# Two row blocks of the last batch moved into the second group of rows, and row scales per two blocks

## The chip, the cores and the metric

The kernel runs on one core of one Trainium2 chip. The metric is the device time of one execution in microseconds, from the runs of the kernel; the profile is one further execution with the hardware profiler on. PE is the matrix engine (PEld its weight loads), DVE the vector engine, ACT the scalar engine, POOL GpSimd, SP the engine that issues the DMAs.

## The reference, cut to what matters

Two stages, for 4 batches, 8 heads of 64 columns and 768 positions. The first is a decayed linear attention; its output, all heads side by side, is `x` of 4 x 768 x 512. The second mixes `x` by a Fourier transform and sends it through a small network:

```python
# first stage, per batch and head, over t:
state = gamma * state + outer(k[t], v[t]);  y[t] = scale * q[t] @ state
# second stage:
X = np.fft.fft(x, axis=1); X = np.fft.fft(X, axis=2)
u  = x + np.real(X)
un = (u - mean(u)) / np.sqrt(var(u) + 1e-06)      # over the 512 columns
out = u + np.maximum(un @ w_ch1, 0.0) @ w_ch2     # 512 -> 2048 -> 512
```

## The kernel before

The 768 rows of a batch are six blocks of 128 rows (`kb` 0 to 5). The program is one core's, and for the last batch the order of the work is set in three steps: lists of units ("streams") are given a start and an end in units of one batch; `emit` sorts all units by their times, which fixes the order in which they are written down; a scheduler under it then sets each engine's instruction order, near to the written one. Each engine then works strictly in its order, and an instruction waits by semaphores for what it reads and for the buffers that it overwrites.

The units that the change and the prediction speak of, with the lines of the kernel before:

- `s2_unit(b, kb)` makes `u` of one block: four matmuls `pq` (L1010), two ACT copies `qn` of the sine parts (L1012, L1013), two DVE instructions that put the parts together (L1017, L1020), and two POOL additions of `x` (L1038, L1040). It is the last step of the Fourier transform. Blocks 3 to 5 are the mirror images of the first three in the sequence's frequencies.
- `norm_unit(b, kb)`: statistics of `u` on DVE (L1050, L1051), then `un = mean - u` on ACT in 16 bits (L1052). It is not divided by the deviation here.
- `unT_unit(b, kb)`: a transposing DMA of `un` into `unT`, issued by SP (L1071).
- `rstd_unit(b, rt)`: the row scales, 1/sqrt(var + eps), by a Sqrt on ACT (L1062) and a reciprocal on DVE (L1064), of three blocks at a time. The scale is applied where the network's output is added to `u`.
- `ch_unit`: the second matrix product of the batches before the last, with L1131 on DVE as its end.

The last batch has no attention work of a next batch beside it. Its network runs over three groups `g` of two blocks each (256 rows), and the second matrix product is done by seven products of half size instead of eight:

- `hp_unit(b, g, n)`, n = 0 to 7: eight matmuls (L1175) into one of three PSUM buffers (`psh`, pool `ps_pm`), then a Relu on ACT (L1180); for n = 7 the second half of the Relu is on DVE (L1183). After n = 2, 5 and 7 DVE makes four sums and differences of the results (L1193).
- `p_unit(b, g, k)`, in the order k = 1, 4, 5, 6, 2, 7, 3: eight matmuls (L1217) and the additions into `u` or into the output buffer on DVE (L1222). Products 1 and 2 share a PSUM bank, so do 6 and 7, and 5 and 3; the second of a pair is accumulated on the first's result after DVE has read that. Stores to `out` go through SP.

```python
# the last batch, before:
for g in range(3):
    majors += [hp_unit(b, g, n) for n in range(8)]
    if g < 2:
        majors.append(rstd_unit(b, g))
    majors += [p_unit(b, g, k) for k in (1, 4, 5, 6, 2, 7, 3)]
```

In the kernel before, blocks 3, 4 and 5 of every batch are put down by `mix_units` with the times `DM1`: for the last batch their three `s2_unit` fall between the hp units of group 0, each norm follows the next block's `s2_unit`, and all is done within group 0. Blocks 0 to 2 are made during the batch before. Group 0 reads blocks 0 and 1, group 1 blocks 2 and 3, group 2 blocks 4 and 5.

Of the kernel before, what the change touches and what calls it, by code (L numbers as in the profile page):

```python
# [20 lines left out]
B, H, S, D = 4, 8, 768, 64  # L21
# [28 lines left out]
DM0, DM1 = (0.183, 0.205, 0.286, 0.408), (0.004, 0.137, 0.232, 0.341)  # L50
# [4 lines left out]
HT0 = (0.666, 0.693, 0.632, 0.590)  # L55
NPE = 2
WS = (-0.12, -0.02)
KD = (2, 3)
NT = 0.6
ACT_ROWS = ((2, 5, 6, 7, 8, 9, 10, 14), (0, 3, 6, 7, 9, 10, 11, 12, 14, 15))  # L60
# [3 lines left out]
def kernel(  # L64
# [330 lines left out]
    for j in range(2):  # L395
# [6 lines left out]
        t = const.tile([P, 257], f32, tag=f"qn_{j}", name=f"qn_{j}", padded_shape=[P, 260])  # L402
# [201 lines left out]
    def t_unit(b, i):  # L604
        def run():
# [9 lines left out]
            for dst, src in ((qT, q16_of[b, i]), (kT, kd_of[b, i])):  # L615
                if dst is kT and i in KD:
                    nc.sync.dma_start_transpose(kT, src.rearrange("p c h d -> p (c h d)"))
# [248 lines left out]
    def g0_unit(b, parts=(0, 1, 2)):  # L866
        def run():
            for part in parts:
                (g0_a, g0_b, g0_c)[part](b)
        return run  # L870
# [79 lines left out]
    def bn_unit(kb):  # L950
        def run():
            stats = lb[0]["st"]
            bst = stt.tile([P, 6], f32, tag=f"bst{kb % 3}", name="bst")
            nc.vector.bn_stats(bst, lb[0]["u"][:, kb, :])
            nc.vector.bn_aggr(stats[:, kb, 0:2], bst)
        return run
# [87 lines left out]
    def norm_unit(b, kb):  # L1044
        def run():
            u, stats = lb[b]["u"], lb[b]["st"]
            bst = stt.tile([P, 6], f32, tag=f"bst{kb % 3}", name="bst")
            un = unp.tile([P, 2, 257], f16, tag="un16", name="un16").rearrange(
                "p a b -> p (a b)")[:, 0:DM]
            nc.vector.bn_stats(bst, u[:, kb, :])  # L1050
            nc.vector.bn_aggr(stats[:, kb, 0:2], bst)  # L1051
            nc.scalar.activation(un, u[:, kb, :], AF.Identity, bias=stats[:, kb, 0:1], scale=-1.0)  # L1052
            lb[b]["un", kb] = un
        return run

    def rstd_unit(b, rt):
        def run():
            stats = lb[b]["st"]
            if b == 0 and rt == 0:
                bn_unit(0)()  # L1060
            sl = slice(3 * rt, 3 * rt + 3)
            nc.scalar.activation(stats[:, sl, 2:3], stats[:, sl, 1:2], AF.Sqrt, bias=epsT,  # L1062
                                 scale=1.0)
            nc.vector.reciprocal(out=stats[:, sl, 3:4], in_=stats[:, sl, 2:3])  # L1064
        return run

    def unT_unit(b, kb):
        def run():
            un, unT = lb[b].pop(("un", kb)), lb[b]["unT"]
            if b > 1 or b and kb >= 3:  # L1070
                nc.sync.dma_start_transpose(unT[:, :, kb * P:(kb + 1) * P], un)  # L1071
                return
            pst = ps_g.tile([P, 4, P], f16, tag="g", name="pst", padded_shape=[P, 8, P])
            for cb in range(4):
                nc.tensor.transpose(pst[:, cb, :], un[:, cb * P:(cb + 1) * P], ident16)
            if (kb % 2 == 0) != (b == 0 and kb < 3):
                nc.vector.tensor_copy(unT[:, :, kb * P:(kb + 1) * P], pst)
            else:
                nc.scalar.copy(unT[:, :, kb * P:(kb + 1) * P], pst)
        return run  # L1080
# [84 lines left out]
    def hp_unit(b, g, n):  # L1165

        def run():
            unT = lb[b]["unT"]
            if (g, n) == (0, 0):
                seven["s4"] = spare(8 * P, "s4").rearrange("p (n k) -> p n k", n=8)  # L1170
            psh = ps_pm.tile([P, 2, 256], f32, tag="pm", name="psh")
            for t in range(2):
                fb = n + 8 * t
                for cb in range(4):
                    nc.tensor.matmul(psh[:, t], w116[:, cb, fb * P:(fb + 1) * P],  # L1175
                                     unT[:, cb, g * 256:(g + 1) * 256],
                                     start=(cb == 0), stop=(cb == 3))
            for t0, t1, eng in (((0, 1, "a"), (1, 2, "v")) if n == 7 else ((0, 2, "a"),)):
                if eng == "a":
                    nc.scalar.activation(hg[:, n, t0:t1], psh[:, t0:t1], AF.Relu, bias=0.0,  # L1180
                                         scale=-1.0)
                else:
                    nc.vector.tensor_scalar(out=hg[:, n, t0:t1], in0=psh[:, t0:t1], scalar1=-1.0,  # L1183
                                            scalar2=0.0, op0=ALU.mult, op1=ALU.max)
            if n in (2, 5, 7):
                sl = slice({2: 0, 5: 3, 7: 6}[n], n + 1)
                a11, a12 = hg[:, sl, 0, 0:P], hg[:, sl, 1, 0:P]
                a21, a22 = hg[:, sl, 0, P:256], hg[:, sl, 1, P:256]
                s1, s2, s4 = sg[:, 0, sl], sg[:, 1, sl], seven["s4"][:, sl]
                for out_, x, y, op in ((s1, a21, a22, ALU.add), (s2, s1, a11, ALU.subtract),  # L1190
                                       (s4, a12, s2, ALU.subtract),
                                       (a21, a11, a21, ALU.subtract)):
                    nc.vector.tensor_tensor(out=out_, in0=x, in1=y, op=op)  # L1193
        return run
# [167 lines left out]
    def mix_units(b, kbs, s0, s1, u0, u1):  # L1362
        def turn(j):
            def run():
                s2_unit(b, kbs[j])()
                if j:
                    norm_unit(b, kbs[j - 1])()
            return run
        t = s1 + NT * min((s1 - s0) / 3, u1 - s1)
        return [([turn(j) for j in range(3)], s0, s1), ([norm_unit(b, kbs[2])], t, t),  # L1370
                ([unT_unit(b, kb) for kb in kbs], u0, u1)]
# [21 lines left out]
    streams = []  # L1393
    for b in range(B):
        majors = []
        if b == B - 1:
            for g in range(3):
                majors += [hp_unit(b, g, n) for n in range(8)]
                if g < 2:
                    majors.append(rstd_unit(b, g))  # L1400
                majors += [p_unit(b, g, k) for k in (1, 4, 5, 6, 2, 7, 3)]
            streams.append(([held(wsum_unit(k, part)) for part in range(2) for k in (1, 2, 3, 4)],
                            b + WS[0], b + WS[1]))
        elif b == 0:
            for kb in range(3):
                if kb:
                    majors.append(unT_unit(0, kb))
                majors += [h0_unit(kb, g) for g in range(4)]
        else:
            majors += [h_unit(b, 0, fb) for fb in range(NFB)]  # L1410
        if b < B - 1:
            majors.append(rstd_unit(b, 0))
            majors += [ch_unit(b, 0, rb3, part) for rb3 in range(3) for part in range(4)]
            majors += [h_unit(b, 1, fb) for fb in range(NFB)]
            majors.append(rstd_unit(b, 1))
            majors += [ch_unit(b, 1, rb3, part) for rb3 in range(3) for part in range(4)]
        streams.append((majors, b, b + 1.0))
        streams += mix_units(b, [3, 4, 5], *(b + t for t in (DM0 if b == 0 else DM1)))
        if b + 1 < B:
            steps = attn_steps(b + 1)  # L1420
            if b == 0:
                streams.append(([load_unit(1, i, 6) for i in range(4)], LD0[0], LD0[1]))
                streams.append(([qt_zeros], 0.1, 0.15))
                streams.append(([half_tables], HT0[0], HT0[1]))
                streams.append(([pad_unit], HT0[2], HT0[3]))
                ts = TS0
            else:
                streams.append(([load_unit(b + 1, i) for i in range(4)], b + LD1[0], b + LD1[1]))
                n = [len(u) for u in steps[1:]]
                ts = list(TS1[:2]) + [TS1[2] + TS1[3] * sum(n[:j]) / sum(n) for j in range(6)]  # L1430
            streams.append((steps[0], b + ts[0], b + ts[1]))
            streams += [(u, b + ts[j + 2], b + ts[j + 3]) for j, u in enumerate(steps[1:])]
            end = b + ts[-1]
            da = DA0 if b == 0 else DA1
            sums = [s1_unit(b + 1, e, cb) for cb in range(2) for e in range(2)]
            sums.insert(1, g0_unit(b + 1, (1, 2)))
            streams.append((sums, end + da[0], end + da[1]))
            streams += mix_units(b + 1, [0, 1, 2], *(end + t for t in da[2:]))
# [31 lines left out]
```

## Time and profile before

| what | value |
|---|---|
| median of 3 runs | 241.73 us (241.58 to 241.75) |
| the profiled execution | 241.30 us |
| its span, first to last instruction | 239.4 us |
| PE busy | 226.8 us, 95% |
| DVE busy | 189.6 us, 79% |
| ACT busy | 125.2 us, 52% |
| POOL busy | 81.6 us, 34% |
| granted TensorE clock | 0.998 |

The span is counted from the first instruction; all times in the views are us from there. A line of a timeline gives start, length, engine, source line, operation, output and inputs, form, count, and in brackets the idle time of the engine before it with what ended that. An instruction's length is from its start to its last write; the next on the same engine starts a little before that end.

### The profile page before, as it was taken

What the parts mean: (1) busy time and instruction counts of PE and PEld (TensorE: products, weight loads), DVE (VectorE), ACT (ScalarE), POOL (GpSimd) and SP (SyncE); (2) the same over time, 40 slices, a digit from 0 to 9 for tenths busy, and PEclk for the clock granted to TensorE, in tenths of its full rate; (3) what the DMA queues carried; (4) which work ended last, traced back from release to release, by engine and by line L of the source; (5) the groups of instructions that cost most, each with busy time, mean ns of one, the idle gap of its engine ahead of it and who ended that gap; (6) DMA issues with size and microseconds to landing.
All of it is one profiled execution on the core that took longest, in us unless ns stands there. A gap on an engine that the chain in (4) does not pass through costs nothing.

```text
span 239.4 us, 5574 instructions
## 1 busy us (share of the span) xinstructions
PE 226.8 (95%) x2127; PEld 155.5 (65%) x2127; DVE 189.6 (79%) x472; ACT 125.2 (52%) x272; POOL 81.6 (34%) x148
## 2 busy tenths in 40 slices
PE   0899999999999999999999999999999998999994
PEld 0376779756775646765567446655675476788883
DVE  8789987968898889986995739977886888848473
ACT  5989758675865544841248406822356337152430
POOL 8378802575300097850001817930003203200000
PEclk9999999999999999999999999999999999999999
DMA  7999999999999289979999487675100240220202
GB/s 181 231 271 238 231 206 208 220 250 248 251 222 227 49 196 213 198 144 136 258 279 216 96 184 204 130 121 153 44 3 0 71 131 22 47 88 1 90 0 88
DMA packets 101242, 36.78 MB, mean 154 GB/s; under 512 B 91489, under 2 KB 98529, under 8 KB 101217
## 3 DMA queue, kind: packets, MB, share of 16 engines
q1 hardware_dynamic: 96992, 32.25, 63.4%
q0 software_dynamic: 4224, 4.19, 10.6%
q8 instruction: 16, 0.26, 0.5%
q14 instruction: 10, 0.07, 0.1%
HBM read 27.26 MB, written 6.29 MB: 140 GB/s over the span
## 4 chain that ended last, share of the span: by engine, by line
PE 85%; DVE 7%; ACT 2%; DMA 2%; issue 1%; POOL 1%; SPq 0%; DVEq 0%; ACTq 0%
PE psc L1127 25%; PE psh L1088 21%; PE psh L1175 7%; PE ps L1217 7%; PE psh L1105 3%; PE wkA L665 3%; PE ps L848 3%; PE ps L828 2%; PE wkY L719 2%; DMA k<-in_k_dram 2%; PE pq L1010 1%; PE wkY L715 1%; PE wkK L684 1%; PE wps L172 1%; PE pq L922 1%
## 5 line engine op out<-in xcount | busy, mean ns | idle before, releaser
L1127 PE MATMUL psc<-w,ht 128*128 128x512 f16 x288 | 67.7, 379 | 0.0
L1088 PE MATMUL psh<-unT,w 128*128 128x384 f16 x320 | 59.5, 326 | 0.0
L1038 POOL TENSOR_TENSOR u<-u,x 128x256 f32<-128x256 f32 x21 | 13.3, 635 | 109.9 <-DVE u L1017 97.5
L1127 PEld LDWEIGHTS <-ht 128*128 128x128 f16 x288 | 27.3, 98 | 26.5
L1088 PEld LDWEIGHTS <-w 128*128 128x128 f16 x320 | 29.9, 98 | 15.9 <-DMA unT<-un 0.4
L1092 ACT ACTIVATE ht<-psh 128x384 f16<-128x384 f32 x46 | 22.3, 489 | 23.4 <-PE psh L1088 22.7
L668 DVE TENSOR_TENSOR atm<-wkA,maskp 128x512 f16<-128x512 f32 x36 | 23.6, 683 | 1.5 <-PE wkA L665 1.5
L1180 ACT ACTIVATE ht<-psh 128x512 f16<-128x512 f32 (+1 forms) x24 | 13.7, 570 | 20.2 <-PE psh L1175 20.2
L1052 ACT ACTIVATE un<-u,stats 128x512 f16<-128x512 f32 x21 | 14.8, 719 | 14.2 <-DVE stats L1051 8.3
L1175 PE MATMUL psh<-unT,w 128*128 128x256 f16 x192 | 22.3, 273 | 0.0
L1094 DVE TENSOR_SCALAR ht<-psh 128x384 f16<-128x384 f32 x34 | 18.7, 551 | 2.7 <-PE psh L1088 2.5
L1175 PEld LDWEIGHTS <-w 128*128 128x128 f16 x192 | 18.7, 98 | 2.3
L1131 DVE SCALAR_TENSOR_TENSOR ob<-psc,stats,u 128x512 f32<-128x512 f32 x18 | 13.4, 744 | 8.2 <-PE psc L1127 7.9
L694 DVE SCALAR_TENSOR_TENSOR s<-s,gk,wkK 128x128 f16<-128x128 f16 x48 | 16.2, 338 | 2.4 <-ACT s L690 1.6
L727 ACT ACTIVATE x<-wkY,gexp 128x384 f16<-128x384 f32 x24 | 12.9, 580 | 9.0 <-PE wkY L719 8.9
L1050 DVE BATCH_NORM_STATS2 bst<-u 128x6 f32<-128x512 f32 x21 | 14.4, 688 | 3.9 <-POOL u L1040 3.7
L1217 PEld LDWEIGHTS <-ht 128*128 128x128 f16 x144 | 13.7, 98 | 4.0 <-ACT ht L1180 1.8
L1193 DVE TENSOR_TENSOR ht<-ht 128x384 f16<-128x384 f16 (+1 forms) x27 | 8.8, 353 | 8.3 <-ACT ht L1180 8.0
L439 POOL TENSOR_SCALAR kd<-k,gexp 128x384 f16<-128x384 f32 x24 | 13.8, 585 | 3.7 <-DMA k<-in_k_dram 3.5
L1040 POOL TENSOR_TENSOR u<-u,x 128x256 f32<-128x256 f32 x21 | 13.4, 640 | 0.0
L665 PE MATMUL wkA<-qTz,kT 128*128 128x256 f16 x72 | 13.2, 272 | 0.0
L1217 PE MATMUL ps<-wsum,ht 128*128 128x256 f16 x96 | 11.8, 273 | 0.1
(190 smaller groups left out, 398.7 us busy)
## 6 DMA issues: line engine op xcount, KB each, us to landing
q<-in_q_dram SPq DMA_DIRECT2D x16, 384.0 KB, 6.0
k<-in_k_dram SPq DMA_DIRECT2D x16, 384.0 KB, 5.7
v<-in_v_dram SPq DMA_DIRECT2D x16, 384.0 KB, 5.9
out_dram<-ob SPq DMA_DIRECT2D x21, 256.0 KB, 2.7
w<-in_moe_w_ch_dram POOLq DMA_DIRECT2D x8, 512.0 KB, 10.8
out_dram<-ob SPq DMA_DIRECT2D x5, 128.0 KB, 2.0
unT<-un SPq DMA_TRANSPOSE x15, 2.5
kT<-kd SPq DMA_TRANSPOSE x10, 2.9
```

The lines of the kernel that those rows point to most:

```text
L439: kc = nc.gpsimd.tensor_scalar(out=kd[:, :, h2, :], in0=k32[:, h2], scalar1=gkd[:, h0 + h2:h0 + h2 + 1], scalar2=1.0, op0=ALU.mult, op1=AL ...
L665: mm = nc.tensor.matmul(wk[:, c2], st["kT"][:, c, :], st["qT"][:, :, c, :], start=True, stop=True)
L668: nc.vector.tensor_tensor(out=st["atm"][:, 2 * part:2 * part + 2], in0=wk, in1=maskp[:, PAIR_ORDER[i]].unsqueeze(1).to_broadcast([P, 2, 2, ...
L694: nc.vector.scalar_tensor_tensor(out=s16[:, c], in0=s16[:, c - 1], scalar=gk2[:, hp:hp + 1], in1=wk[:, c - c0], op0=ALU.mult, op1=ALU.add)
L1050: nc.vector.bn_stats(bst, u[:, kb, :])
L1052: nc.scalar.activation(un, u[:, kb, :], AF.Identity, bias=stats[:, kb, 0:1], scale=-1.0)
L1088: nc.tensor.matmul(psh, w116[:, cb, fb * P:(fb + 1) * P], unT[:, cb, rt * 384:(rt + 1) * 384], start=(cb == 0), stop=(cb == 3))
L1092: nc.scalar.activation(ht16[:, fb, :], psh, AF.Relu, bias=0.0, scale=-1.0)
L1094: nc.vector.tensor_scalar(out=ht16[:, fb, :], in0=psh, scalar1=-1.0, scalar2=0.0, op0=ALU.mult, op1=ALU.max)
L1127: nc.tensor.matmul(psc, ht16[:, fb, rb3 * P:(rb3 + 1) * P], w216[:, fb, :], start=(fb == 0), stop=(fb == NFB - 1))
L1175: nc.tensor.matmul(psh[:, t], w116[:, cb, fb * P:(fb + 1) * P], unT[:, cb, g * 256:(g + 1) * 256], start=(cb == 0), stop=(cb == 3))
L1217: nc.tensor.matmul(ps[:, c0:c1], lhsT, rhs[:, c0:c1], start=bool(new and n == 0), stop=(n == 7), skip_group_check=True)
```

## The change

In the last batch blocks 3, 4 and 5 no longer come from `mix_units`: each unit gets a time of its own. One batch is 48 units long there (three times 8 hp, one scale unit, 7 products), so block 3's `s2_unit` at 0.02 stands ahead of the first hp unit, its norm at 0.06 after the second, its transpose at 0.15; block 4's `s2_unit` at 0.36 stands after the first hp unit of group 1, its norm at 0.41 and transpose at 0.50; block 5's at 0.42, 0.47 and 0.56. The row scales of the last batch are made for two blocks at a time, three times, after the hp units of each group; before, they were made for three blocks, twice.

```diff
+LAST_MIX = {3: (0.02, 0.06, 0.15), 4: (0.36, 0.41, 0.50), 5: (0.42, 0.47, 0.56)}
...
-    def rstd_unit(b, rt):
+    def rstd_unit(b, rt, n=3):
...
-            sl = slice(3 * rt, 3 * rt + 3)
+            sl = slice(n * rt, n * rt + n)
...
                 majors += [hp_unit(b, g, n) for n in range(8)]
-                if g < 2:
-                    majors.append(rstd_unit(b, g))
+                majors.append(rstd_unit(b, g, 2))
                 majors += [p_unit(b, g, k) for k in (1, 4, 5, 6, 2, 7, 3)]
...
-        streams += mix_units(b, [3, 4, 5], *(b + t for t in (DM0 if b == 0 else DM1)))
+        if b < B - 1:
+            streams += mix_units(b, [3, 4, 5], *(b + t for t in (DM0 if b == 0 else DM1)))
+        else:
+            streams += [([unit(b, kb)], b + t, b + t) for kb, ts in LAST_MIX.items()
+                        for unit, t in zip((s2_unit, norm_unit, unT_unit), ts)]
```

## The prediction

> **What bounds the kernel now.** I read the page, then the stages of the last batch by window, then the timelines of PE, ACT, DVE and POOL there. The page's first lines and its row of transposes:
>
> ```profile
> span 239.4 us, 5574 instructions
> PE 226.8 (95%) x2127; PEld 155.5 (65%) x2127; DVE 189.6 (79%) x472; ACT 125.2 (52%) x272; POOL 81.6 (34%) x148
> ...
> unT<-un SPq DMA_TRANSPOSE x15, 2.5
> ```
>
> PE is the bound, so only PE's gaps and PE's instruction count can move the time. The count stays (the same matmuls in another order). The windows, cut at the three groups of rows (stage, length, then busy PE, PEld, DVE, ACT, POOL):
>
> ```profile
> 193.68:209.44 15.76, 14.33 (x133) 12.11 (x132) 13.09 (x35) 7.70 (x18) 3.80 (x6) 1.00 0.18 47
> 209.44:222.54 13.10, 13.10 (x122) 11.71 (x120) 8.33 (x22) 4.55 (x8) 0.00 (x0) 1.00 0.13 46
> ```
>
> PE's timeline (start, length, count, idle before):
>
> ```profile
> 193.68 1.91 PE L1175 MATMUL psh<-unT,w 128*128 128x256 f16 x16
> 195.43 0.40 PE L1010 MATMUL pq<-gk,g16r 128*128 128x129 f16 x4
> 195.66 1.91 PE L1175 MATMUL psh<-unT,w 128*128 128x256 f16 x16
> ...
> 202.49 0.28 PE L1217 MATMUL ps<-w,ht 128*128 128x256 f16 x1 [0.31 <-ACT ht L1180]
> 203.76 0.28 PE L1217 MATMUL ps<-w,ht 128*128 128x256 f16 x1 [0.99 <-ACT ht L1180]
> ...
> 209.77 6.82 PE L1175 MATMUL psh<-unT,w 128*128 128x256 f16 x61
> 216.43 1.04 PE L1217 MATMUL ps<-w,ht 128*128 128x256 f16 x8
> ...
> 222.54 7.15 PE L1175 MATMUL psh<-unT,w 128*128 128x256 f16 x64
> ```
>
> Group 1 is gapless: 64 matmuls of hp and 56 of p in 13.10 us, 0.109 each. (Three of its 64 run inside group 0, hence 209.77 - 3 x 0.109 = 209.44.) A block's four pq matmuls take 195.66 - 195.43 = 0.23. So group 0's 15.76 us is 13.10 + 3 x 0.23 + **1.96 us of waiting**, and the change can win no more. Who is waited for:
>
> ```profile
> 194.76 0.60 ACT L1180 ACTIVATE ht<-psh 128x512 f16<-128x512 f32 x1 [5.20 <-PE psh L1175]
> 195.63 0.60 ACT L1180 ACTIVATE ht<-psh 128x512 f16<-128x512 f32 x1 [0.28 <-PE psh L1175]
> 196.12 0.27 ACT L1012 COPY qn<-pq 128x128 f32<-128x128 f32 x1
> 196.27 0.29 ACT L1013 COPY qn<-pq 128x127 f32<-128x127 f32 x1
> ...
> 200.90 0.72 ACT L1052 ACTIVATE un<-u,stats 128x512 f16<-128x512 f32 x1 [0.71 <-DVE stats L1051]
> ...
> 202.72 0.72 ACT L1052 ACTIVATE un<-u,stats 128x512 f16<-128x512 f32 x1 [0.28 <-issue]
> 203.35 0.36 ACT L1180 ACTIVATE ht<-psh 128x256 f16<-128x256 f32 x1
> ```
>
> ACT works in order. A block's `un` waits there for its DVE and POOL chain, and the Relus of hp stand behind it: the Relu of n=7 ends at 203.71 and PE goes on at 203.76.
>
> **The change part by part.** Read from the changed program's instruction order. PE: block 3's pq, 64 hp, 56 p; then 8 hp, pq 4, 24 hp, pq 5, 32 hp, 56 p; group 2 as before. ACT from group 0 on (Relus by n):
>
> ```
> g0: qn3 | R0 R1 | un3 | R2 | sqrt | R3..R7
> g1: R0 | qn4 | R1 R2 R3 | un4 | qn5 | R4..R7 | un5 | sqrt
> ```
>
> DVE in group 1: u4, stats4, one L1193, aggr4, three L1193, u5, one L1193, stats5, three L1193, aggr5, Relu of the second half of n=7 (L1183), then the old order, with a reciprocal ahead of the add of product 6. So group 0 loses two blocks, but both groups now have an `un` in the middle of the Relus. The chain of each block is priced from these rows of DVE, and of POOL behind them:
>
> ```profile
> 194.71 0.75 DVE L1131 SCALAR_TENSOR_TENSOR ob<-psc,stats,u 128x512 f32<-128x512 f32 x1
> 196.60 0.48 DVE L1017 SCALAR_TENSOR_TENSOR u<-pq,g,qn 128x256 f32<-128x256 f32 x1 [1.15 <-ACT qn L1013]
> 197.39 0.62 DVE L1193 TENSOR_TENSOR ht<-ht 128x384 f16<-128x384 f16 x1
> 200.56 0.17 DVE L1051 BATCH_NORM_AGGREGATE stats<-bst 128x2 f32<-128x6 f32 x1
> 201.59 0.70 DVE L1050 BATCH_NORM_STATS2 bst<-u 128x6 f32<-128x512 f32 x1 [0.86 <-POOL u L1040]
> 202.20 0.34 DVE L1193 TENSOR_TENSOR ht<-ht 128x384 f16<-128x384 f16 x1
> 202.46 0.18 DVE L1051 BATCH_NORM_AGGREGATE stats<-bst 128x2 f32<-128x6 f32 x1
> 202.58 0.63 DVE L1193 TENSOR_TENSOR ht<-ht 128x384 f16<-128x384 f16 x2
> 208.65 0.17 DVE L1064 RECIPROCAL stats<-stats 128x3 f32<-128x3 f32 x1
> 217.10 0.42 DVE L1183 TENSOR_SCALAR ht<-psh 128x256 f16<-128x256 f32 x1
> 219.03 1.66 DVE L1222 SCALAR_TENSOR_TENSOR u<-ps,stats,u 128x256 f32<-128x256 f32 x4
> ```
>
> ```profile
> 197.16 0.64 POOL L1038 TENSOR_TENSOR u<-u,x 128x256 f32<-128x256 f32 x1 [10.02 <-DVE u L1017]
> 197.75 0.75 POOL L1040 TENSOR_TENSOR u<-u,x 128x256 f32<-128x256 f32 x1
> 200.92 0.64 POOL L1040 TENSOR_TENSOR u<-u,x 128x256 f32<-128x256 f32 x1
> ```
>
> *Group 0, after.* pq 3 is ready early, but block 3's u stands behind the last L1131 of batch 2, which starts at 194.71; the next DVE instruction starts about 0.09 before it ends: 195.37. POOL +0.56 (196.60 to 197.16): 195.93; its second add +0.59 and 0.64 long, done 197.16. stats +0.03 (201.56 to 201.59): 197.19, 0.70 long; aggr 197.93 to 198.10; un3 +0.17 (200.73 to 200.90): 198.27; R2 +0.63 (202.72 to 203.35): 198.90, done 199.50. Three psh buffers: hp n=5 needs the one that R2 frees, so PE starts it at 199.55 (+0.05, as at 203.71). Its turn is at 193.68 + 0.23 + 40 x 0.109 = 198.28. **Stall 1.27.** Behind it PE's own pace ends last again: R7 and L1183 come as soon as hp n=7 is done, and p finds its operands as in group 1 of before, which has no gap. Group 0 ends at 193.68 + 0.23 + 13.10 + 1.27 = 208.28.
>
> *Group 1, after,* in us from its start T = 208.28. R0 1.08 (193.68 to 194.76), qn4 1.57 (+0.49), u4 2.05 (+0.48, 196.12 to 196.60), POOL 2.61, its second add 3.20 to 3.84, stats4 3.87, aggr4 4.74 (+0.87, 201.59 to 202.46, one L1193 between, as here), done 4.92, un4 5.00 (+0.08, 202.64 to 202.72), qn5 5.63, u5 6.11, POOL 6.67, its second add 7.26 to 8.01 (0.75, the row in which L1193 ran beside it; here it does too), stats5 8.04, L1193 8.65 (+0.61), three steps of 0.27 to aggr5 9.46, L1183 9.58 (+0.12). The Relus held by un4 and qn5 do not stop hp: R4 runs from 5.94 to 6.54, and hp n=7, which needs its buffer, has its turn at 56 x 0.109 + 0.46 = 6.57. Then p: PE reaches p at 64 x 0.109 + 2 x 0.23 = 7.45, and product 4's n=7, its 16th matmul, at 9.09. That one reads what L1183 writes: 9.58 + 0.42 + 0.05 = 10.05. **Stall 0.96.** DVE is now behind with the rest. In before product 1's second add ends 2.41 after L1183's start (219.03 + 0.48 - 217.10), product 6's add 3.59 after it (219.03 + 1.66), now plus 0.1 for the reciprocal (0.17 less the overlap). PE overwrites these banks with products 2 and 7. Product 2: turn 10.05 + 17 x 0.109 = 11.90, free at 12.04: 0.13. Product 7: turn 12.04 + 0.87 = 12.91, free at 13.27 + 0.05: **0.41**. Group 1 takes 13.10 + 0.46 + 1.50 = 15.06 and ends at 223.34.
>
> *Group 2* starts at 222.54 before, so the sum is **+0.80**; or 2.77 us of stalls for 1.96. It needs block 5's transpose: un5 starts at T + 9.72, done 218.7, plus 2.5 for a landing: 221.2, 2.1 us in hand (that is the cover; with none, each us later would be a us). On SP the transposes of 4 and 5 stand behind group 0's stores, whose data are ready by 209, and ahead of group 1's, whose first comes later than un5. Of the row scales there is one Sqrt and one reciprocal more (three of 128x2 for two of 128x3 in this batch); the reciprocal is in the sum, and the Sqrt stands after R2, where ACT has slack until n=7. Does a third Sqrt among Relus reload a table?
>
> ```profile
> L1062 ACT ACTIVATE stats<-stats,epsT x8: 283/286/300, 48.5 to 206.9; 128x3 f32<-128x3 f32 x8
> L1062 ACT ACT_TABLE_LOAD  x1: 1283/1283/1283, 47.2 to 47.2; - x1
> ```
>
> Eight, one load: no. The bounds of what the rows leave open: un waits 0.08 to 0.17 behind aggr (two uns: 0.2 us either way), POOL's second add 0.64 or 0.75 (0.11 less), the reciprocal 0 to 0.18. Together about 0.4 to 1.1.
>
> The profiled execution took 241.30 (span 239.4), the median of the runs is 241.73; on its scale 242.1, on the runs' 241.73 + 0.80 = **242.5**. A measurement can tell 0.2% here, 0.48 us.
>
> **The rivals.** *POOL and DVE shut each other out whole.* In before L1193 at 197.39 overlaps both POOL adds and takes 0.62 for the 0.34 of the row at 202.20; it ends 198.01. If it waited out the first add (197.80) it would end at 198.14, and the second add, waiting in turn, at 198.78, not 198.50. So partly slowed, not shut out. Shut out, L1193 in group 1 (ready at about T + 7.05) waits for 7.31, ends 7.65, the add ends 8.29 for 8.01: +0.28, 242.8. Chance 0.07. The Trainium skill, SBUF — State Buffer, "Who interferes with whom", says that two-input DVE instructions and GpSimd reads exclude each other for a whole instruction; by that rule 242.8 would stand, and these rows disagree with it in part.
>
> *It cancels.* Every link above is a single reading. If L1183 comes at T + 9.2 instead of 9.6, products 4, 2 and 7 all lose 0.4 and the sum is +0.4; with un3 0.1 earlier, +0.3: 242.0, no change. For it: PE is late by little at each point. Against: none of the links runs shorter elsewhere in the rows by so much. Chance 0.16.
>
> *Faster: group 1 swallows the blocks.* ACT is busy 4.55 and DVE 8.33 of its 13.10 us; two blocks add about 2.6 and 3.7, which fits. If un4 and un5 found their stats ready, no Relu would be held, L1183 would come by T + 8.6, where the stall of 0.96 ends, and with block 3 as quick 1.96 us would go: 239.8; half of that is still faster. Against: busy time is not the limit, the in-order waits are, and both un4 and u5 wait on POOL inside group 1. Chance 0.09. That the blocks do not move is excluded by the order.
>
> **How the numbers follow.** Forecast 0.68, shutting out 0.07, cancelling 0.16, faster 0.09. Slower by over 0.2%: 0.75; within: 0.16; faster: 0.09. The range leaves out the faster case and the tails: from 241.8 (cancelling) to 243.1 (shutting out plus the upper bound).
>
> **What would show it.** In the profile after: a gap of 1.2 to 1.3 on PE at hp n=5 of group 0 released by ACT; group 0 done near 208.3; in group 1 gaps at product 4 (near 1.0) and product 7 (near 0.4) released by DVE; group 2 from 223.3; no wait for unT. Wrong, if group 1 has no gap, if group 0 keeps its 1.96, or if group 2 starts before 222.5.

## The result, and the profile after

The changed kernel takes 242.34 us (median of 22 runs) beside 241.81 us for the kernel before (22 runs): ratio 1.0025, 95% interval 1.0016 to 1.0033, so 0.4 to 0.8 us more. It is slower, by about as much as can be told from no change. The profiled execution took 242.68 us with a span of 240.8; group 0 begins there at 194.39, not 193.68. Of these 0.71 us, 0.65 are one wait of PE for a DMA, long before the changed code; PE of the kernel after:

```profile
116.63 0.38 PE L666 MATMUL wkA<-qTz,kT 128*128 128x256 f16 x2 [0.65 <-DMA qTz<-q16z]
```

The profile of the kernel before shows no wait at that place, and those of the experiments below between none and 0.61 us. It is not counted; only the two groups are compared.

The windows of the kernel after, cut at the starts of group 0 (with block 3's pq), 1 and 2 (columns as before):

```profile
194.39:208.94 14.55, 13.48 (x125) 11.95 (x124) 10.65 (x28) 5.55 (x12) 1.23 (x2) 1.00 0.15 51
208.94:223.92 14.98, 14.07 (x131) 12.07 (x129) 10.77 (x31) 6.64 (x15) 2.58 (x4) 1.00 0.21 58
```

Group 0 went from 15.76 to 14.55 us, group 1 from 13.10 to 14.98: together 28.86 before and 29.53 after, +0.67. The matmuls of the two groups and three pq fill 2 x 13.10 + 3 x 0.23, or 26.9 us, so PE waited 1.96 us before and 2.63 after. Where, by PE's timeline of the kernel after:

```profile
194.62 4.53 PE L1176 MATMUL psh<-unT,w 128*128 128x256 f16 x40
200.22 2.78 PE L1176 MATMUL psh<-unT,w 128*128 128x256 f16 x24 [1.07 <-ACT ht L1181]
...
217.32 0.93 PE L1218 MATMUL ps<-wsum,ht 128*128 128x256 f16 x7
218.96 2.03 PE L1218 MATMUL ps<-wsum,ht 128*128 128x256 f16 x17 [0.71 <-DVE ht L1184]
220.94 1.03 PE L1218 MATMUL ps<-w,ht 128*128 128x256 f16 x8
222.17 1.03 PE L1218 MATMUL ps<-wsum,ht 128*128 128x256 f16 x8 [0.20 <-DVE u L1223]
223.92 1.26 PE L1176 MATMUL psh<-unT,w 128*128 128x256 f16 x10
```

Each gap counts from the turn (the row's start plus its matmuls at 0.109): hp n=5 was due at 198.98 and began at 200.22; product 4's n=7 was due at 218.08 and began at 218.96; product 2 was 0.13 late, product 7 0.36. Lines are one higher than in the kernel before: L1181 is the Relu, L1184 its second half for n=7, L1223 the additions.

What held them, on ACT, then DVE, then POOL of the kernel after:

```profile
196.56 0.60 ACT L1181 ACTIVATE ht<-psh 128x512 f16<-128x512 f32 x1 [0.28 <-PE psh L1176]
198.96 0.72 ACT L1053 ACTIVATE un<-u,stats 128x512 f16<-128x512 f32 x1 [1.80 <-DVE stats L1052]
199.59 0.58 ACT L1181 ACTIVATE ht<-psh 128x512 f16<-128x512 f32 x1
...
213.99 0.72 ACT L1053 ACTIVATE un<-u,stats 128x512 f16<-128x512 f32 x1 [0.47 <-DVE stats L1052]
```

```profile
195.40 0.74 DVE L1132 SCALAR_TENSOR_TENSOR ob<-psc,stats,u 128x512 f32<-128x512 f32 x1
196.06 0.47 DVE L1018 SCALAR_TENSOR_TENSOR u<-pq,g,qn 128x256 f32<-128x256 f32 x1
197.88 0.69 DVE L1051 BATCH_NORM_STATS2 bst<-u 128x6 f32<-128x512 f32 x1 [0.95 <-POOL u L1041]
...
216.05 0.43 DVE L1194 TENSOR_TENSOR ht<-ht 128x384 f16<-128x384 f16 x1
217.01 0.70 DVE L1051 BATCH_NORM_STATS2 bst<-u 128x6 f32<-128x512 f32 x1 [0.53 <-POOL u L1041]
...
218.42 0.17 DVE L1052 BATCH_NORM_AGGREGATE stats<-bst 128x2 f32<-128x6 f32 x1
218.51 0.39 DVE L1184 TENSOR_SCALAR ht<-psh 128x256 f16<-128x256 f32 x1
```

```profile
215.63 0.64 POOL L1039 TENSOR_TENSOR u<-u,x 128x256 f32<-128x256 f32 x1 [2.80 <-DVE u L1018]
216.23 0.75 POOL L1041 TENSOR_TENSOR u<-u,x 128x256 f32<-128x256 f32 x1
```

ACT stands idle for 1.80 us in front of un3 while the matmuls that R2 is to read have long ended (the Relu before began at 196.56, the next matmuls took 0.87). In group 1 DVE waits 0.53 for POOL in front of block 5's stats, and all that is queued behind, the second half's Relu at 218.51 among it, comes late.

### The profile page after: what moved, and what is told of

The parts are those of the page before. It is cut to its first block, busy times and chain, and to the rows that moved or that the text cites. A ratio compares the mean times of both kernels' runs of the same rounds, so it can differ in the third digit from the quotient of the medians.

```text
span 240.8 us, 5577 instructions
## 1 busy us (share of the span) xinstructions
PE 226.5 (94%) x2127; PEld 155.1 (64%) x2127; DVE 189.6 (79%) x473; ACT 125.3 (52%) x273; POOL 81.6 (34%) x148
## 4 chain that ended last, share of the span: by engine, by line
PE 76%; DVE 8%; DMA 6%; ACT 3%; POOL 3%; issue 1%; SPq 1%; POOLq 0%; DVEq 0%; ACTq 0%
PE psc L1128 23%; PE psh L1089 21%; PE ps L1218 6%; PE psh L1176 4%; PE psh L1106 3%; PE wkA L666 3%; DMA qTz<-q16z 3%; DMA v<-in_v_dram 3%; PE ps L849 3%; PE wkY L720 2%; PE pq L1011 2%; PE ps L829 1%; PE wkY L716 1%; PE wkK L685 1%; PE pq L923 1%
## 5 line engine op out<-in xcount | busy, mean ns | idle before, releaser
L1181 ACT ACTIVATE ht<-psh 128x512 f16<-128x512 f32 (+1 forms) x24 | 13.4, 570 | 16.1 <-PE psh L1176 16.0
L1132 DVE SCALAR_TENSOR_TENSOR ob<-psc,stats,u 128x512 f32<-128x512 f32 x18 | 13.4, 743 | 8.6 <-PE psc L1128 8.4
L1194 DVE TENSOR_TENSOR ht<-ht 128x384 f16<-128x384 f16 (+1 forms) x27 | 8.3, 334 | 6.3 <-ACT ht L1181 6.0
```

## The experiments

The theory: PE waits because instructions that stand in ACT's and DVE's queues in front of PE's suppliers wait there for POOL; time moves with their places in the queues. The rivals: the row scales cost it; or one engine simply has too much to do in a group. Ratios are to the kernel before, run on the same chip. "Two groups" is the length from the start of group 0 to that of group 2 in the profile, and the gaps are what is left of it without the 26.90 us of matmuls (26.67 where pq 3 lies ahead of group 0; then the gaps, not the lengths, compare with the other rows). A hundredth is within the rounding of the rows.

| kernel | ratio (95% interval) | two groups, us | gaps, us |
|---|---|---|---|
| before | 1 | 28.86 | 1.96 |
| after | 1.0025 (1.0016 to 1.0033) | 29.53 | 2.63 |
| scales only | 0.9995 (0.9982 to 1.0009) | 28.86 | 1.96 |
| block 3 early | 1.0050 (1.0031 to 1.0069) | 29.72 | 3.05 |
| blocks 4 and 5 earlier | 0.9980 (0.9963 to 0.9996) | 28.32 | 1.42 |
| norm 3 behind | 0.9995 (0.9982 to 1.0008) | 28.51 | 1.61 |
| only block 3 moved | 1.0082 (1.0064 to 1.0101) | 30.34 | 3.44 |
| no POOL additions | 0.9948 (0.9930 to 0.9965) | 27.47 | 0.57 |
| all, scales late | 0.9930 (0.9915 to 0.9945) | 26.91 | 0.01 |
| sums earlier | 1.0026 (1.0012 to 1.0040) | 29.34 | 2.67 |
| norm 3 behind the store | 1.0005 (0.9992 to 1.0019) | 28.52 | 1.85 |

**Scales only.**

```diff
-        if b < B - 1:
+        if b < B:
             streams += mix_units(b, [3, 4, 5], ...)
```

> The blocks stay where they were in the kernel before (mix_units, all three in group 0); only the row scales of the last batch are made for two blocks, three times. Theory (the time moved because un of blocks 3 and 5 is waited for in the middle of the Relus): nothing moves, ratio to the kernel before 1.000 within 0.001, group 0 near 15.8 us with 1.96 us of gaps, group 1 13.1. Rival (the third Sqrt and reciprocal, or the scales' new places, cost the time): 1.0025, the whole of what the change cost.

The two groups take the same 28.86 us as before, with the same gaps at the same places. The scales cost nothing that can be measured; the rival is out.

**Block 3 early.**

```diff
-LAST_MIX = {3: (0.02, 0.06, 0.15), ...}
+LAST_MIX = {3: (-0.04, -0.01, 0.15), ...}
```

> The changed kernel with block 3's pq put ahead of the last 12 matmuls of batch 2, so that its u on DVE stands ahead of two of the eight sums of the weights and of the last L1131 (L1132 there) instead of behind them; blocks 4 and 5 as in the changed kernel. Theory: un3 is ready some 2 us earlier and no longer holds R2, the 1.23 us gap at hp n=5 goes, groups 0 and 1 keep the rest: 1.2 us less than the changed kernel, ratio to the kernel before 0.9975 (0.9965 to 0.9985). Rival (group 0 is held by its load on DVE as a whole, which moves only to other places): a gap of a similar size elsewhere in group 0 or at the last matmuls of batch 2, ratio 1.001 to 1.003.

A miss: a gap elsewhere in group 0, as the rival has it, and more time than the rival gave (1.0050 for 1.001 to 1.003). PE of this kernel, and DVE:

```profile
198.13 1.03 PE L1176 MATMUL psh<-unT,w 128*128 128x256 f16 x8 [0.89 <-DVE ob L1132]
199.60 3.65 PE L1176 MATMUL psh<-unT,w 128*128 128x256 f16 x32 [0.43 <-ACT ht L1181]
```

```profile
194.83 0.95 DVE L1162 TENSOR_TENSOR wsum<-w 128x1024 f16<-128x1024 f16 x1
195.71 1.12 DVE L1162 TENSOR_TENSOR wsum<-w,wsum 128x1024 f16<-128x1024 f16 x1
196.75 0.68 DVE L1051 BATCH_NORM_STATS2 bst<-u 128x6 f32<-128x512 f32 x1
197.35 0.73 DVE L1132 SCALAR_TENSOR_TENSOR ob<-psc,stats,u 128x512 f32<-128x512 f32 x1
```

A new wait: hp n=3 needs the PSUM bank that the last L1132 of batch 2 frees (the psc banks and the psh banks are the same three), and that L1132 now stands behind block 3's stats and behind two sums of the weights that took 0.95 and 1.12 us in place of 0.69. Which of the two did it, the last two experiments ask.

**Blocks 4 and 5 earlier.**

```diff
-LAST_MIX = {..., 4: (0.36, 0.41, 0.50), 5: (0.42, 0.47, 0.56)}
+LAST_MIX = {..., 4: (0.30, 0.38, 0.45), 5: (0.36, 0.43, 0.50)}
```

> The changed kernel with block 4 put into the products of group 0 (its pq after product 2) and block 5 into block 4's old place in group 1 (its pq after hp n=0); block 3 as in the changed kernel. The work on each engine is the same. Theory: un5 comes where un4 came, its stats no longer stand ahead of the second half's Relu of n=7, the three gaps of group 1 (0.87, 0.12, 0.36 us) go and group 0's 1.23 stays: 1.35 us less than the changed kernel, ratio to the kernel before 0.997 (0.996 to 0.998). Rival (group 1 has too much DVE work in all): the gap at product 4 goes but the ones at products 2 and 7 of either group grow, ratio 1.000 to 1.002.

As the theory has it: 1.21 us less than the change in the two groups. PE in the products of group 1:

```profile
217.21 2.78 PE L1218 MATMUL ps<-wsum,ht 128*128 128x256 f16 x24
219.82 1.04 PE L1218 MATMUL ps<-w,ht 128*128 128x256 f16 x8
220.90 1.03 PE L1218 MATMUL ps<-wsum,ht 128*128 128x256 f16 x8
```

Group 1's gap at product 4 is gone and 0.2 is left at product 7; the 1.24 of group 0 stays to the hundredth. The work of the two groups together is the same. The two instructions that make block 4's u (about 0.9 us of DVE) left group 1, its statistics stayed, so by itself this run does not exclude that DVE had too much to do there. "No POOL additions" below does: DVE has all the work of both blocks in group 1, 10.87 us of 13.90, and the gaps at products 4, 2 and 7 are gone.

**Norm 3 behind.**

```diff
-LAST_MIX = {3: (0.02, 0.06, 0.15), ...}
+LAST_MIX = {3: (0.02, 0.127, 0.15), ...}
-            streams += [([unit(b, kb)], b + t, b + t) ...
+            streams += [([held(unit(b, kb)) if (unit, kb) == (norm_unit, 3)
+                          else unit(b, kb)], b + t, b + t) ...
```

> The changed kernel with only the norm of block 3 held back in the order: its stats stand behind the second four L1193 of group 0 (L1194 there) and un3 behind R7. pq 3, u and the POOL adds come at the same time as in the changed kernel, so the chain of block 3 is not quicker, it is only not in front of a Relu. Theory: the 1.23 us gap goes; the stats ahead of the second half's Relu of n=7 and the reciprocal cost DVE some 0.3 us there, which comes back as up to 0.3 us at product 7: 0.9 to 1.2 us less than the changed kernel, ratio to the kernel before 0.998 (0.997 to 0.9990). Rival (the gap comes from PE or POOL work of block 3 itself, not from un's place in ACT's order): 1.002 to 1.003 as the changed kernel.

PE of this kernel:

```profile
194.73 7.15 PE L1176 MATMUL psh<-unT,w 128*128 128x256 f16 x64
...
205.21 1.04 PE L1218 MATMUL ps<-w,ht 128*128 128x256 f16 x8
206.29 1.03 PE L1218 MATMUL ps<-wsum,ht 128*128 128x256 f16 x8
```

The 64 hp matmuls run without a gap, though u of block 3 is no earlier: the norm's place in the queues made the gap. (The edit moves its statistics on DVE too, but PE waited for the Relu behind un, on ACT.) 0.21 comes back at product 7, as forecast. The two groups lose 1.02 us against the change; the ratio fell by 0.3%, 0.7 us. At 0.9995 it lies outside the expected 0.997 to 0.9990, though its interval, which begins at 0.9982, reaches into that range. The 0.35 us that the two groups lose against the kernel before is 0.9986, inside both.

**Only block 3 moved.**

```diff
-LAST_MIX = {..., 4: (0.36, 0.41, 0.50), 5: (0.42, 0.47, 0.56)}
+LAST_MIX = {..., 4: (0.093, 0.137, 0.28), 5: (0.137, 0.164, 0.33)}
```

> The row scales per two blocks and block 3 as in the changed kernel, blocks 4 and 5 in group 0 near their old places (pq 4 after hp n=3, pq 5 after n=5). Theory (each un in the middle of the Relus costs its own wait): un3 holds R2 as in the changed kernel (1.2 us), un4 then holds R7 and so product 1, and un5 and its stats come into the first products: group 0 has 2.7 to 3.7 us of gaps, group 1 none: ratio to the kernel before 1.003 to 1.007. Rival (block 3's early place is what costs, and 4 and 5 in group 0 are harmless once it is out of their way): group 0 with 1.2 us of gaps, ratio 0.997.

PE of this kernel (three of its gaps), and ACT in front of the second:

```profile
200.06 1.03 PE L1176 MATMUL psh<-unT,w 128*128 128x256 f16 x8 [0.84 <-ACT ht L1181]
205.24 0.28 PE L1218 MATMUL ps<-w,ht 128*128 128x256 f16 x1 [1.40 <-ACT ht L1181]
207.95 1.05 PE L1218 MATMUL ps<-wsum,ht 128*128 128x256 f16 x8 [0.29 <-DVE ht L1194]
```

```profile
204.19 0.72 ACT L1053 ACTIVATE un<-u,stats 128x512 f16<-128x512 f32 x1 [1.36 <-DVE stats L1052]
204.82 0.36 ACT L1181 ACTIVATE ht<-psh 128x256 f16<-128x256 f32 x1
```

Gaps of 3.44 us, as the theory summed them, un4 in front of the Relu of n=7 as forecast. The runs are a little slower still than the forecast 1.007. So of the change's two halves, giving block 3 its early place costs about 1.5 us (this kernel against the scales alone, where pq 4 and 5 stand at the same places among PE's matmuls, while the norms of 4 and 5 stand a little differently), and taking 4 and 5 out of group 0 wins back 0.8.

**No POOL additions.** The two additions of `x` are left out for blocks 3 to 5 of the last batch.

```diff
             x = xts[b % 2]
+            if b == B - 1 and kb >= 3:
+                return
             nc.gpsimd.tensor_tensor(out=u[:, kb, 0:256], ...
```

> The changed kernel with the two POOL additions of x left out for blocks 3, 4 and 5 of the last batch (u lacks x there); DVE, ACT and PE keep all their work, and the order differs only in that the scheduler puts un4 before R3 and un5 before R7. Theory (the chains of un wait on POOL, not on a lack of time on ACT or DVE): each chain is 1.2 us shorter or more, the 1.23 us gap falls to 0.2 or less, those of group 1 to 0.3 together: 2.0 to 2.4 us less than the changed kernel, ratio to the kernel before 0.993 to 0.995. Rival (DVE has too much to do in group 1): group 1 keeps its 1.35 us, ratio 0.998.

PE of this kernel (its lines behind the edit are two higher than in the kernel after):

```profile
193.76 7.38 PE L1178 MATMUL psh<-unT,w 128*128 128x256 f16 x64
...
215.65 0.28 PE L1220 MATMUL ps<-w,ht 128*128 128x256 f16 x1 [0.17 <-ACT ht L1183]
```

0.57 us of gaps are left, 0.23 in group 0 and 0.34 at product 1 of group 1. DVE, ACT and PE had all their work; taking POOL's link out of three chains took away three quarters of the gaps.

**All of it, and the scales late.** Edits of the two kernels "blocks 4 and 5 earlier" and "norm 3 behind", and:

```diff
-                majors.append(rstd_unit(b, g, 2))
-                majors += [p_unit(b, g, k) for k in (1, 4, 5, 6, 2, 7, 3)]
+                if g == 0:
+                    majors.append(rstd_unit(b, g, 2))
+                majors += [p_unit(b, g, k) for k in (1, 4, 5, 6, 2)]
+                if g < 2:
+                    majors.append(held(rstd_unit(b, g + 1, 2)))
+                majors += [p_unit(b, g, k) for k in (7, 3)]
```

> Blocks 4 and 5 earlier as in e3, block 3's norm held behind R7 as in e7, and the row scales of group 1 and 2 put behind product 2 of the group before. Theory: gaps of group 0 and 1 together 0.3 us or less against 1.96 in the kernel before, 2.58 in the changed one: 1.7 to 2.0 us less than the kernel before, ratio 0.992 (0.991 to 0.993), about 239.9 us. Rival (the gains of e3 and e7 overlap, since both only hand DVE's work on): 0.996.

The windows of this kernel:

```profile
193.97:207.53 13.56, 13.56 (x130) 12.20 (x128) 10.70 (x30) 6.36 (x14) 1.74 (x3) 1.00 0.18 58
207.53:220.88 13.35, 13.35 (x126) 11.93 (x124) 10.43 (x29) 6.08 (x13) 1.95 (x4) 1.00 0.20 56
```

PE has no gap in either group: 240.04 us against 241.77 for the kernel before, the quickest of all. Each engine does the same work in the two groups together as in the change; what differs is the places in the queues: block 4's pq stands among the products of group 0, block 5's just ahead of group 1's hp units, and the norm of block 3 and the scales stand later. The ratio is at the upper edge of the expected 0.991 to 0.993.

**Sums earlier.** The edit of "block 3 early", and:

```diff
-WS = (-0.12, -0.02)
+WS = (-0.24, -0.13)
```

> e2 again (block 3's pq ahead of the last 12 matmuls of batch 2) with the eight sums of the weights (L1161, L1162 there) put earlier, so that they are over when block 3's POOL adds run. In e2 two of them ran against POOL's adds and took 0.95 and 1.12 us for 0.69, and the last L1132 stood behind them and gave its PSUM bank late. Theory (e2 failed by that): un3 comes 2 us earlier, no gap in group 0: ratio to the kernel before 0.9975 (0.9965 to 0.9985). Rival (block 3 cannot be made early at all, something else held e2): 1.003 to 1.005 as e2.

The second miss. PE and DVE of this kernel:

```profile
197.64 5.40 PE L1176 MATMUL psh<-unT,w 128*128 128x256 f16 x48 [1.09 <-DVE ob L1132]
```

```profile
185.76 0.87 DVE L1162 TENSOR_TENSOR wsum<-w 128x1024 f16<-128x1024 f16 x1
...
186.95 0.72 DVE L1162 TENSOR_TENSOR wsum<-w,wsum 128x1024 f16<-128x1024 f16 x1
...
196.24 0.69 DVE L1051 BATCH_NORM_STATS2 bst<-u 128x6 f32<-128x512 f32 x1 [0.94 <-POOL u L1041]
196.85 0.73 DVE L1132 SCALAR_TENSOR_TENSOR ob<-psc,stats,u 128x512 f32<-128x512 f32 x1
```

The sums are out of the way of block 3, and the gap stays, now 1.26 us at hp n=2: DVE waits 0.94 for POOL in front of block 3's stats, and L1132 stands behind. My explanation of the miss before was wrong in its main part.

**Norm 3 behind the store.** The same with one edit: `3: (-0.04, 0.001, 0.15)` and the norm of block 3 `held`, so that its stats stand behind the last L1132.

> e9 with one edit: the stats of block 3 stand behind the last L1131 (L1132 there) on DVE, not ahead of it. In e9 they stood ahead, waited there for POOL until 196.24, and the last L1132 of batch 2, whose PSUM bank hp n=2 needs, came at 196.85: the gap of 1.26 us is at hp n=2, released by L1132, and not by un3. Theory (e2 and e9 were held by that order, not by the sums of the weights against POOL): L1132 comes near 195.2 on e9's scale, the gap at n=2 goes; un3 near 197.2 stands ahead of R1 in this order, so hp n=4 may wait 0.4 us for R1's bank: group 0 takes 13.1 to 13.6 us against 14.4 in e9, ratio to the kernel before 0.9985 (0.9975 to 0.9995). Rival (block 3 made before group 0 costs as much anywhere): gap of 1.2 us somewhere else in group 0, ratio 1.002 to 1.003.

```profile
198.71 3.65 PE L1176 MATMUL psh<-unT,w 128*128 128x256 f16 x32 [0.29 <-ACT ht L1181]
```

That settles the gap of "sums earlier": at n=2 it is gone, the 0.46 at n=4 was foretold as 0.4, group 0 takes 13.55. In "block 3 early" the sums had their part too, since they ran 0.69 us longer ahead of the stats. The ratio is 1.0005, outside the 0.9975 to 0.9995 of the expectation, which I had converted badly: the two groups with pq 3 come to 28.75 us, 0.78 less than in the change but only 0.11 less than before, which is 0.9995 and inside the interval.

## Why the prediction was right, point by point

The forecast was 242.5 us and +0.80; measured were 242.34 us, +0.67 in the two groups and +0.4 to +0.8 in the runs. The case that carried 0.68 of the chance came, with its gaps at the places and from the engines that it named, each a little smaller than forecast. The interval of the runs alone would hardly tell it from the cancelling case (+0.4); the gaps in the profile do.

- *Group 0's gap at hp n=5 through un3 and R2:* forecast 1.27, measured 1.24; un3 4.59 us after the group's start forecast, 4.57 measured. Shown by "norm 3 behind", where that gap goes and only 0.21 comes back at product 7.
- *Group 1 through L1183:* forecast 9.58 after the group's start, measured 9.57 (L1184, 218.51). Gaps at products 4, 2 and 7: forecast 0.96, 0.13, 0.41, measured 0.88, 0.13, 0.36. PE came to p at 7.51, not 7.45, and L1184 took 0.39, not 0.42: these two make the difference at product 4. The 0.06 by which PE came late is a small gap within hp, where the prediction had none ("do not stop hp"). Shown by "blocks 4 and 5 earlier", where of these gaps only the 0.2 at product 7 is left.
- *Nothing waits for block 5's transpose:* it is issued at 219.4, the slowest of the three took 2.5 us to land, and group 2 starts at 223.92 without a gap, some 2.0 us after the landing (forecast 2.1). The tile's answer and the line of the scales, kernel after:

```profile
L1072 SPq DMA_TRANSPOSE unT<-un x3: 1190/1196/1196, 199.7 to 219.4; - x3
...
DMA to landing us min/median/max: 2.3/2.4/2.5
```

```profile
L1063 ACT ACTIVATE stats<-stats,epsT x9: 282/285/301, 48.5 to 219.3; 128x3 f32<-128x3 f32 x6, 128x2 f32<-128x2 f32 x3
L1063 ACT ACT_TABLE_LOAD  x1: 1283/1283/1283, 47.2 to 47.2; - x1
```

- *No reload for the third Sqrt:* nine Sqrts (eight before) and still one table load; "scales only" measures no cost.
- *POOL and DVE shutting each other out:* here I read the trace wrong. It did the sum no harm, which was partly luck: I had copied the 0.75 of the row for the second addition, and it came at 0.75 again. The rows of the kernel after say more: the first addition ends at 216.27, L1194 at 216.48, 0.21 behind it where it needs some 0.35 alone; the second addition ends at 216.98, 0.50 behind L1194 where it needs 0.64. Each ends as if it had waited for the other's end, with only some 0.14 of its length before that end; the first addition, which came first, kept its 0.64. "Partly slowed" is not what happens: they do shut each other out, and the rival's +0.28 had charged those 0.14 twice over, so that the true price of its mechanism was the one already in the forecast. The Trainium skill, SBUF — State Buffer, "Who interferes with whom", has the rule of the exclusive lock; these rows agree with it but for the 0.14.
- *Cancelling and faster:* neither came, and "all, scales late" shows what the second would have needed: the norms at other places. That ACT and DVE had room in group 1 was right and beside the point.

What stays open: "only block 3 moved" is slower by 0.1 to 1.0 us more than its two groups explain (1.48 us or 0.61%, against a ratio of 1.0064 to 1.0101).

## What to carry to other kernels

On an engine that works in order, price a moved step by when its inputs are ready at its place in each queue, and by what stands behind it there; free time on the engine does not tell. A chain through a slow helper (here 1.2 us of POOL between two DVE instructions) belongs into the queue behind what could run meanwhile, unless it is ready by its turn, and where three PSUM banks are used in turn, an instruction that frees a bank should not stand behind it. A replay of the new order, by hand, with lengths and hand-over times from the rows of the old trace, gave the gaps of the changed kernel to within 0.1 us. It is only as good as the list of what is followed: the expectation of "block 3 early" did not follow the bank that the last L1132 frees, that of "sums earlier" not DVE's wait for POOL in front of that L1132, and they missed gaps of 1.05 and 1.26 us.

## What the runs showed of the hardware that was not expected

DVE's additions of two f16 operands in SBUF (L1162, L1194) and POOL's additions exclude each other almost whole. POOL of the kernel "sums earlier", beside its DVE rows above:

```profile
185.44 0.64 POOL L1039 TENSOR_TENSOR u<-u,x 128x256 f32<-128x256 f32 x1 [1.19 <-DVE u L1018]
186.04 1.08 POOL L1041 TENSOR_TENSOR u<-u,x 128x256 f32<-128x256 f32 x1
187.10 1.06 POOL L1039 TENSOR_TENSOR u<-u,x 128x256 f32<-128x256 f32 x1
```

The ends alternate: POOL 186.08, DVE 186.63, POOL 187.12, DVE 187.67, POOL 188.16. Each comes 0.55 (DVE, 0.69 alone) or 0.49 (POOL, 0.64 alone) behind the other's. The DVE instructions of s2_unit that read one operand from PSUM kept their length beside POOL: L1018 at 186.55, between the sums and beside the addition that ends at 187.12, took 0.47, as alone.
